# First products of eight f-tiles from scaled fp16 parts, and score visits that take two tiles, in a fused attention and feed-forward kernel on one core

## The chip, the cores and the metric

The kernel runs on one core of one Trainium2 chip. The metric is the device time in microseconds (us) of one execution, the median of several; lower is better. The kernel issues work on TensorE (PE in the rows; PEld is its weight load), VectorE (DVE), ScalarE (ACT), GpSimd (POOL), and DMAs from SyncE's queue (SP).

## What is computed

Linear attention memory and causal softmax attention are mixed by a gate, and the result goes through a feed-forward layer with softplus:

```python
# q, k, v: (4, 8, 576, 64); w_in: (512, 2048), w_out: (2048, 512); fp32 in and out
scores = where(causal, -1e9, 0.125 * q @ k.T)
a = exp(scores - max); a /= a.sum() + 1e-9
local = a @ v
q_p = elu(q) + 1
mem_out = (q_p @ M_prev) / (q_p @ z_prev + 1e-6)
x = sigmoid(beta) * mem_out + (1 - sigmoid(beta)) * local     # then (2304, 512)
out = softplus(x @ w_in) @ w_out
```

The weights arrive as 64-bit words and are turned into fp32 on the core ("decode").

## The kernel before

**Numbers as parts.** A fp32 operand of the feed-forward layer is kept as two fp32r parts, a high one and a low one (`hi`, `lo`), and a product is three matmuls: high by high, high by low, low by high (`in_pairs`, `out_pairs`, `mms`, L384). The attention weights and v are kept as two fp16 parts in most windows.

**Attention.** There are 16 units (4 batches by 4 pairs of heads), each cut into two windows: A has query chunks 0 and 1, B has chunks 2, 3 and the half chunk 4. `chunks` issues for each chunk a score visit on PE (fp32 matmuls of 64 by 64 quarters of the array, four at a time, L529; then a mask is added by two bf16 matmuls, L540 or L544), the row maxima (DVE, L549), the exponentials (ACT, L560), the high and low fp16 parts (POOL L617, DVE L621) and a transposing DMA. Chunk 4 has 64 queries per head; both heads stand in one 128-wide operand `qz` that POOL builds (L571), and its scores are two full-array matmuls of 288 columns (L533) and a mask (L535). A fp32 matmul stands as two records in the trace, so L533 has four per visit and L529 eight per chunk. Each visit uses one of the two score tiles of ring `s`. `v_prep` finds a power of two for v by a maximum, a tiny matmul pair against a constant (L749, L750) and a few scalar operations (L756, L758). `memory` does the linear memory (L800), `values` the product with v (L838) and the two parts of x (L867, L869).

**Feed-forward.** Its hidden units are 16 f-tiles of 128. f-tiles 0 to 6 are decoded during the attention and stay; for every finished block of x (8 blocks, 256 or 320 rows each, in turn) `fill` runs their first product (`hin`), softplus, and second product and puts the partial result into DRAM (`part`); this is also the work that PE does between attention steps. When the attention's buffers are free, f-tiles 7 to 15 are decoded into their place: one piece of `w_in` and one of `w_out` each, per piece four DVE steps (L349, L356, L360, L364) with one POOL step between them (L353), a cast on ACT (`hi`, L323) and a subtraction on POOL (`lo`, L317). `rest` then runs the last block with all 16 f-tiles and the seven others with f-tiles 7 to 15; there a first product of 12 matmuls (L384) alternates with a second product of 12 (L951).

**What sets the order.** A planner in the kernel (`Plan.run`) simulates the engines with the durations written at each `op`, ranks them by the tables at the top (`DEC`, `RK`, `SLOT`) and writes every engine's instructions in that order, so each engine's queue is fixed before the run. Where PE would idle early, it puts in dummy matmuls (L1034).

Of the kernel before, what the change touches and what calls it, by code (L numbers as in the profile page):

```python
# [10 lines left out]
F32 = mybir.dt.float32  # L11
# [83 lines left out]
class Plan:  # L95
# [5 lines left out]
    TURN = {"m": {"S": 60.0, "v": 160.0, "n": 70.0}, "f": {"v": 85.0}, "n": {"S": 30.0, "v": 80.0},  # L101
            "S": {"S": 85.0, "v": 80.0, "f": 90.0, "m": 90.0, "n": 90.0},
            "v": {"S": 80.0, "f": 90.0, "m": 90.0, "n": 90.0}}
# [44 lines left out]
    def run(self):  # L148
# [34 lines left out]
        def opens(o):  # L183
            t = 0.0
            for h in o.tiles:
                if h.ring is None or h.open:
                    continue
                if h.ring.free:
                    if h.before is not None and not h.before.open:
                        return None  # L190
                    if len(h.ring.opened) >= h.ring.bufs:
                        old = h.ring.opened[-h.ring.bufs]
# [80 lines left out]
def attn_softplus_moe(  # L273
# [25 lines left out]
    own = res.tile([128, 128], F32, name="own")  # L299
# [14 lines left out]
    LASTB = len(blocks) - 1  # L314

# [55 lines left out]
    def wpart(f, i, t):  # L371
        return W[f]()[:, i, t, :]

    def in_pairs(f, xh, kd, n):
        wh, wl = (W[f]()[:, 0, t, kd * 128:(kd + 1) * 128] for t in range(2))
        return [(wh, xh[:, 0, kd, :n]), (wh, xh[:, 1, kd, :n]), (wl, xh[:, 0, kd, :n])]

    def out_pairs(f, g, dm, n):
        wh, wl = (W[f]()[:, 1, t, dm * 128:(dm + 1) * 128] for t in range(2))
        return [(wh, g[:, 0, :n]), (wh, g[:, 1, :n]), (wl, g[:, 0, :n])]  # L380
# [5 lines left out]
    def consts():  # L386
# [11 lines left out]
        P.memset(own, 0.0)  # L398
        for h in range(2):
            P.memset(own[64 * h:64 * h + 64, 64 * h:64 * h + 64], 1.0)  # L400
# [9 lines left out]
        for r in range(2):  # L410
            V.tensor_copy(cinv4[64 * r:64 * r + 64, :], cv[64 * r:64 * r + 64, :, r])
# [12 lines left out]
    def ring(pool, tag, bufs, shape, dtype=F32):  # L424
# [6 lines left out]
        "sm": ring(ps_r, "sm", 1, [128, 512]),  # L431
# [11 lines left out]
        "PTA": ring(al, "PTA", 2, [128, 8, 256], F16), "PTB": ring(al, "PTB", 2, [128, 18, 320], F16),  # L443
# [8 lines left out]
    W = {}  # L452
    for f in range(NF):
# [3 lines left out]
        else:  # L457
            late, old = (wr, gone[ar]) if f < GA + 5 else (wl, gone[al])
            W[f] = Ring(late, f"w{f}", 1, [128, 2, 2, 512], F32R, old).new()
    QZ = [Handle(None, 0) for _ in range(2)]  # L460
    for i, h in enumerate(QZ):
        h.t = res.tile([128, 128], F32, name=f"qz{i}")
    X = [Handle(None, 0) for _ in blocks]
    PART = [Handle(None, 0) for _ in blocks]

    def decode(f, i, rank):
        s, tu = R["ws"].new(), R["wu"].new()
        hi, lo = (W[f], (i, 0)), (W[f], (i, 1))
# [4 lines left out]
        src = tu if WIDE else s  # L473
        for j, (e, d, port, fn) in enumerate(steps):
            if j < nv:
                op(e, d, rank, fn, r=[s], w=[tu], port=port)
            elif j == nv:
# [25 lines left out]
    def chunks(u, win, b, p, cs, ks):  # L503
# [14 lines left out]
        ss, nms, pts = (tiles(t) for t in ("s", "nm", "P"))  # L518
        l, r = R["l"].new(), R["rr"].new()

        def scores(js):
            for j in js:
                c, n, sv, qv, kv = cs[j], ns[j], ss[j](), q()[:, 130:], kk()
                cq = c * 128 - q0
                if c < 4:
                    for h in range(2):
                        rr = slice(64 * h, 64 * h + 64)
                        for e in range(0, 128, 64):
                            MM(sv[e:e + 64, h, so[j]:so[j] + n], lhsT=qv[rr, cq + e:cq + e + 64], rhs=kv[rr, :n],  # L529
                               start=j == js[0], stop=True, skip_group_check=True)  # L530
                else:
                    for i in range(2):
                        MM(sv[:, i, :288], lhsT=win.qz(), rhs=kv[:, 288 * i:288 * i + 288], start=True, stop=True)  # L533
            if m == 1:
                MM(sv[:, 1, 224:288], lhsT=identb, rhs=mask4, start=False, stop=True, skip_group_check=True)  # L535
                return
            for h in range(2):
                e = so[js[-1]] + ns[js[-1]]
                if len(js) == 2:
                    MM(sv[:, h, 0:512].rearrange("p (c n) -> p c n", c=2)[:, :, 0:128], lhsT=identb,  # L540
                       rhs=mask.unsqueeze(1).to_broadcast([128, 2, 128]), start=False, stop=True,
                       skip_group_check=True)
                else:
                    MM(sv[:, h, e - 128:e], lhsT=identb, rhs=mask, start=False, stop=True, skip_group_check=True)  # L544
# [22 lines left out]
        for j, c in enumerate(cs):  # L567
            k, s, nm, pt = ks[j], ss[j], nms[j], pts[j]
            if m == 1:
                win.qz = QZ[win.no // 2 % 2]  # L570
                op("POOL", 470, k + RK["qz"], lambda: P.tensor_tensor(  # L571
                    out=win.qz().rearrange("p (h q) -> p h q", h=2),
                    in0=q()[:, 130 + 256:130 + 320].unsqueeze(1).to_broadcast([128, 2, 64]),
                    in1=own.rearrange("p (h q) -> p h q", h=2), op=ALU.mult), r=[q], w=[win.qz])
            if not both or j == 0:
                js = range(len(cs)) if both else [j]
                op("PE", 1080 if both else (450, 660, 968, 1180, 1050)[c], k, lambda js=js: scores(js),
                   r=[q, kk] + ([win.qz] if m == 1 else []), mode="S" if m == 2 else "f",
                   w=[s] + ([(pt, "s")] if guard else []))
# [24 lines left out]
        for j, c in enumerate(cs):  # L604
            k, pt, phl = ks[j], pts[j], phls[j]
            if c < 4:
# [23 lines left out]
                op("SP", (1230, 1250, 1650, 2600)[c], k + RK["lo"], lambda j=j, c=c, nk=nk: SY.dma_start_transpose(  # L630
                    out=ptw()[:, 0:4 * nk, c * 128 - q0:c * 128 - q0 + 128],
                    in_=phls[j]()[:, ho[j]:ho[j] + nk * 512]),
                   r=[(phl, 4 * j + i) for i in range(4)], w=[(ptw, c)], dma=840 * nk)
# [29 lines left out]
            for h in range(2):  # L663
                op("SP", 1260, k + RK["lo"], lambda h=h: SY.dma_start_transpose(
                    out=ptw().rearrange("p (j h) q -> p j h q", h=2)[:, :, h, 256:320],
                    in_=phl()[64 * h:64 * h + 64, 0:1152]),
# [425 lines left out]
```

## Time and profile before

| | |
|---|---|
| median of 3 runs | 611.39 us (608.29 to 611.94) |
| the profiled execution | 610.6 us, of which the trace spans 608.8 |
| PE busy | 590.4 us (97%) |
| DVE, ACT, POOL busy | 353.0 (58%), 302.4 (50%), 173.0 (28%) |
| chain of work that ended last | 86% PE, of which first products (L384) 43%, second products of `rest` (L951) 21% |
| granted TensorE clock | 2.4 GHz (1.00) from start to end |

Rows of the windows view give, for a stretch, each engine's busy time and number of instructions. Rows of the timeline give start, duration (of the merged run) and count; matmuls are pipelined, so a run's pace is the distance between the starts of two runs divided by the count, not its duration.

### The profile page before, as it was taken

How to read it: one execution, taken by the hardware profiler on the slowest of the kernel's cores; microseconds unless marked ns; L12 is line 12 of the kernel's file. 1: busy time of each engine (PE TensorE's matmuls, PEld its weight loads, DVE VectorE, ACT ScalarE, POOL GpSimd, SP SyncE). 2: the span in 40 equal slices, each digit the busy share in tenths (PEclk: the TensorE clock that was granted, in tenths of full speed). 3: DMA queues.
4: the chain of work that ended last, by engine and by line, in shares of the span. 5: the costliest groups of instructions: out<-in, count | busy, mean ns of one | idle time of the engine just before them, and what ended most of it. 6: DMA issues, size and time to landing. Idle time of an engine off the chain costs nothing.

```text
span 608.8 us, 12824 instructions
## 1 busy us (share of the span) xinstructions
PE 590.4 (97%) x4866; PEld 528.5 (87%) x4866; DVE 353.0 (58%) x805; ACT 302.4 (50%) x854; POOL 173.0 (28%) x262
## 2 busy tenths in 40 slices
PE   6999999999989999989999999999999999999996
PEld 5676768787777787968799999999999999999996
DVE  6688888788877898868882776651212121212121
ACT  5758866666756785668743443432222222222221
POOL 3556533334433435326622343330000000000000
PEclk9999999999999999999999999999999999999999
DMA  8545559868999789967976643342314130522011
GB/s 314 190 125 178 181 157 220 195 195 183 205 180 210 192 187 200 177 164 163 169 123 182 214 137 106 105 145 98 105 36 133 48 132 6 167 71 70 1 44 35
DMA packets 129245, 87.41 MB, mean 144 GB/s; under 512 B 86176, under 2 KB 120992, under 8 KB 129184
## 3 DMA queue, kind: packets, MB, share of 16 engines
q1 hardware_dynamic: 129184, 86.60, 55.3%
q8 instruction: 38, 0.62, 0.4%
q14 instruction: 23, 0.19, 0.1%
HBM read 47.88 MB, written 18.22 MB: 109 GB/s over the span
## 4 chain that ended last, share of the span: by engine, by line
PE 86%; DMA 5%; DVE 4%; ACT 1%; SPq 1%; POOL 1%; issue 1%; DVEq 0%; ACTq 0%; POOLq 0%
PE h L384 43%; PE s L951 21%; PE s L529 6%; PE xp L838 4%; PE sm L800 3%; PE s L533 2%; DMA kA<-in_nat_dram 2%; PE xp L853 2%; PE xp L826 1%; PE s L544 1%; PE h L488 1%; DMA qA<-in_nat_dram 1%; PE s L715 1%; DVE nm L549 1%; DMA PTA<-PHL 1%
## 5 line engine op out<-in xcount | busy, mean ns | idle before, releaser
L384 PE MATMUL h<-xhl,w 128*128 128x256 f32 (+1 forms) x1536 | 228.1, 298 | 1.4 <-ACT pb L914 1.4
L384 PEld LDWEIGHTS h<-xhl,w 128*128 128x128 f32 x1536 | 210.4, 189 | 3.2 <-ACT pb L914 1.6
L317 DVE TENSOR_TENSOR g<-gl,g 128x256 fp32r<-128x256 f32 (+1 forms) x128 | 59.6, 470 | 162.8 <-ACT g L323 162.5
L888 ACT ACTIVATE gl<-h 128x256 f32<-128x256 f32 (+1 forms) x128 | 52.2, 410 | 179.2 <-PE h L384 176.8
L951 PE MATMUL s<-g,w 128*128 128x320 f32 (+1 forms) x948 | 139.3, 297 | 0.0
L951 PEld LDWEIGHTS s<-g,w 128*128 128x128 f32 x948 | 131.1, 188 | 0.0
L384 PE MATMUL h<-g,w 128*128 128x256 f32 (+1 forms) x588 | 87.1, 299 | 0.0
L384 PEld LDWEIGHTS h<-g,w 128*128 128x128 f32 x588 | 78.7, 189 | 0.7
L617 POOL TENSOR_SCALAR PHL<-P,rr 128x384 f16<-128x384 f32 (+3 forms) x100 | 57.4, 589 | 76.9 <-DVE rr L597 23.5
L560 ACT ACTIVATE P<-s,nm 128x256 f32<-128x256 f32 (+3 forms) x128 | 66.4, 526 | 5.2 <-DVE PHL L621 2.6
L549 DVE TENSOR_REDUCE nm<-s 128x2 f32<-128x768 f32 (+2 forms) x64 | 51.4, 818 | 13.9 <-PE s L540 7.3
L323 ACT CAST g<-gl 128x256 fp32r<-128x256 f32 (+1 forms) x128 | 55.1, 433 | 3.9
L621 DVE SCALAR_TENSOR_TENSOR PHL<-P,rr,PHL 128x384 f16<-128x384 f32 (+3 forms) x100 | 56.4, 599 | 0.8 <-POOL PHL L617 0.8
L317 POOL TENSOR_TENSOR w<-wu,w 128x512 fp32r<-128x512 f32 x23 | 30.5, 1329 | 29.2 <-ACT w L323 29.2
L353 POOL TENSOR_SCALAR wu<-wu 128x512 f32<-128x512 f32 x32 | 20.5, 643 | 43.7 <-DVE wu L349 38.3
L529 PE MATMUL s<-kB,qB 64*64 64x384 f32 (+1 forms) x256 | 31.4, 561 | 0.0
L838 PEld LDWEIGHTS <-vb 128*64 128x64 f16 x508 | 24.8, 110 | 7.1 <-issue 2.7
L360 DVE SCALAR_TENSOR_TENSOR wu<-ws,wu 128x512 int32<-128x512 int32 x32 | 26.6, 832 | 0.9
L792 POOL TENSOR_TENSOR ph<-ph,pe 128x320 f32<-128x320 f32 (+1 forms) x22 | 18.4, 838 | 30.8 <-ACT pe L784 18.9
L560 ACT ACTIVATION_READ_ACCUMULATOR P<-s,nm 128x1 f32 x128 | 25.5, 199 | 0.0
L323 ACT CAST w<-wu 128x512 fp32r<-128x512 f32 x29 | 17.9, 618 | 14.4 <-DVE wu L364 14.2
L678 POOL TENSOR_SCALAR P<-P,rr 128x256 f32<-128x256 f32 (+4 forms) x31 | 18.6, 613 | 20.5 <-DVE rr L597 10.7
(123 smaller groups left out, 643.2 us busy)
## 6 DMA issues: line engine op xcount, KB each, us to landing
ws<-in_w_in_dram SPq DMA_DIRECT2D x16, 512.0 KB, 3.6
ws<-in_w_out_dram SPq DMA_DIRECT2D x16, 512.0 KB, 3.5
va<-in_nat_dram SPq DMA_DIRECT2D x16, 320.0 KB, 3.9
xd<-xhl SPq DMA_DIRECT2D x16, 320.0 KB, 3.1
kB<-in_nat_dram SPq DMA_DIRECT2D x16, 288.0 KB, 3.8
xd<-xhl SPq DMA_DIRECT2D x16, 256.0 KB, 3.2
xhl<-xd SPq DMA_DIRECT2D x8, 512.0 KB, 4.6
xhl<-xd SPq DMA_DIRECT2D x6, 640.0 KB, 4.9
```

The costliest lines, as they stand in the source:

```text
L317: eng.tensor_tensor(out=out, in0=in0, in1=in1, op=ALU.subtract)
L323: A.copy(out, in_)
L360: V.scalar_tensor_tensor(out=ti(), in0=si(1), scalar=-0x40000000, in1=ti(), op0=ALU.bitwise_and, op1=ALU.bitwise_or)
L384: MM(out, lhsT=l, rhs=r, start=start and i == 0, stop=stop and i == len(pairs) - 1)
L529: MM(sv[e:e + 64, h, so[j]:so[j] + n], lhsT=qv[rr, cq + e:cq + e + 64], rhs=kv[rr, :n], start=j == js[0], stop=True, skip_group_check=True)
L549: V.tensor_reduce(out=nm()[:, 2 * j * both:2 * j * both + 2], in_=s()[:, :, so[j]:so[j] + n], op=ALU.max, axis=AX.X, negate=True)
L560: A.activation(out=pt()[:, po[j] + h * n:po[j] + h * n + n], in_=s()[:, h, so[j]:so[j] + n], func=AF.Softplus, scale=SCALE, bias=nm()[:, o ...
L617: P.tensor_scalar(out=o[:, :, 0, h, :], in0=src, scalar1=rs, scalar2=0.0, op0=ALU.mult, op1=ALU.add)
L621: V.scalar_tensor_tensor(out=o[:, :, 1, h, :], in0=src, scalar=rs, in1=o[:, :, 0, h, :], op0=ALU.mult, op1=ALU.subtract)
L838: MM(xp()[64 * h:64 * h + 64, lo:n], lhsT=vb()[:, vi, kc, 64 * h:64 * h + 64], rhs=ptw()[:, kc * 4 + t * 2 + h, lo:n], start=False, stop=( ...
L888: op("ACT", 170 + .833 * n, -1, lambda: A.activation(out=gl()[:, :n], in_=hp()[:, :n], func=AF.Softplus, scale=XSC), r=[hp], w=[gl])
L951: MM(bank(dm), lhsT=l, rhs=r, start=f == f0 and q == 0 and (not small or dm % 2 == 0), stop=f == NF - 1 and q == 2, skip_group_check=True)
```

## The change

- **First products of f-tiles 8 to 15** (`FINE`) use fp16 parts in place of fp32r parts. Each decoded `w_in` piece is scaled by a power of two found from its absolute maximum (`spread`: one DVE reduction, two tiny matmuls on PE, three one-column DVE operations); ACT writes the high fp16 part and DVE (not POOL) the low one. For each of the 8 blocks `halved` does the same to x: a reduction, the tiny matmuls, one ACT pass and two DVE passes over 4 times 256 or 320 columns, and one one-column DVE operation per f-tile that gives the softplus its inverse scale. Second products stay in fp32r, and so do f-tiles 0 to 7.
- **Chunk 4** of two neighbouring units is computed in one visit (`fours`), on 64 by 64 quarters, both units' quarters side by side; `qz` and its POOL operation are gone. The first unit's chunk 4 and values come after the second unit's chunk 3 scores.
- **Chunks 2 and 3** of 14 units are computed in one visit (`twos`). A visit of either kind takes both tiles of ring `s`.
- **Masks** are now written by the first matmuls of a visit, and the scores are added to them.
- The two transposing DMAs of a window A are one. The second memory product is split for 12 windows instead of 10 (`PHS`). Later `w_out` pieces have their own load and decode buffers (`ws2`, `wu2`). Some casts and evictions change engine; the planner's costs of switching PE between kinds of work (`TURN`) and the tables `DEC`, `RK`, `SLOT` have other numbers, so that the whole order is drawn anew.

The core of the diff:

```diff
+    def spread(src, out, rank, r, w, dur, axis):
+        sp = R["sm"].new(loose=True)
...
+        op("DVE", dur, rank, lambda: V.tensor_reduce(out=total(), in_=src(), op=ALU.max, axis=axis,
+                                                     apply_absolute_value=True), r=r, w=[(w, 3)])
+        op("PE", 80, rank, mn, r=[(w, 3)], w=[sp], mode="n")
+        op("DVE", 450, rank, scale, r=[sp], w=[(w, 1)])
...
     def decode(f, i, rank):
-        s, tu = R["ws"].new(), R["wu"].new()
+        s, tu = (R[g + "2" * (f > GA and i)].new() for g in ("ws", "wu"))
...
+                if j == nv:
+                    spread(raw, sf, rank, [src], WS[f], 690, AX.X)
+                    op("ACT", 640, rank, lambda: A.activation(out=wpart(f, 0, 0), in_=raw(), func=AF.Copy,
+                                                              scale=sf()[:, 1:2]), r=[src, (WS[f], 1)], w=[hi])
+                else:
+                    op("DVE", 740, rank, lambda: V.scalar_tensor_tensor(
+                        out=wpart(f, 0, 1), in0=raw(), scalar=sf()[:, 1:2], in1=wpart(f, 0, 0), op0=ALU.mult,
+                        op1=ALU.subtract), r=[src, hi, (WS[f], 1)], w=[lo], port=True)
...
+    def fours(wins, ks):
+        ss = [R["s"].new() for _ in wins]
...
+            for s in ss:
+                MM(s()[:, 1, 224:288], lhsT=identb, rhs=mask4, start=True, stop=False, skip_group_check=True)
+            for i in (1, 0):
+                for h in range(2):
+                    rr = slice(64 * h, 64 * h + 64)
+                    for s, w in zip(ss, wins):
+                        o = 64 * (h ^ w.odd)
+                        MM(s()[o:o + 64, i, :288], lhsT=w.q()[rr, 130 + 256:130 + 320],
+                           rhs=w.k()[rr, 288 * i:288 * i + 288], start=i == 0, stop=True, skip_group_check=True)
...
+    def halved(xh, n, rank):
...
+        spread(lambda: part(0), xs, rank, xr[:4], xs, 150 + 4.16 * n, AX.XY)
+        op("ACT", 260 + 3.36 * n, rank, lambda: A.activation(out=out(0), in_=part(0), func=AF.Copy,
+                                                             scale=xs()[:, 1:2]), r=xr[:4] + [(xs, 1)], w=[(x, 0)])
+        op("DVE", 215 + 4.16 * n, rank, lambda: V.scalar_tensor_tensor(
+            out=out(1), in0=part(0), scalar=xs()[:, 1:2], in1=out(0), op0=ALU.mult, op1=ALU.subtract),
+           r=xr[:4] + [(xs, 1), (x, 0)], w=[(x, 1)], port=True)
+        op("DVE", 215 + 4.16 * n, rank, lambda: V.scalar_tensor_tensor(
+            out=out(1), in0=part(1), scalar=xs()[:, 1:2], in1=out(1), op0=ALU.mult, op1=ALU.add),
+           r=xr[4:] + [(xs, 1)], w=[(x, 1)], port=True)
...
-        for f in range(f0, NF):
+        fs = [f for f in range(f0, NF) if f not in FINE] + FINE
+        for f in fs:
...
-            g = hin(f, xh, n, k + i)
+            g = hin(f, xh, n, k + i, fine if f in FINE else None)
...
+        if w == "B" and win.odd:
+            ks = [key(0), key(1)]
+            both = fours([prev[1], win], ks)
+            chunks(*prev, [4], ks[:1], both[0])
+            chunks(u, win, b, p, [4], ks[1:], both[1])
+            slot += 2
+            values(*prev, slot + RK["val"], xhs[2 * b + 1])
+        pre = twos(win, [key(0), key(1)]) if w == "B" and u.no in OPT["two"] else None
```

Two places of the order. First TensorE's queue in the last batch of the attention. Before: a visit for chunk 3 (tile `kB`, 512 columns), other work, and a visit for chunk 4 of one unit (with `qz`).

```order
L529 MATMUL s<-kB,qB 64x512 x4
L544 LDWEIGHTS identb
L544 MATMUL s<-mask,identb 128x128
L544 LDWEIGHTS identb
L544 MATMUL s<-mask,identb 128x128
L800 MATMUL sm<-qB,ph 128x130 x3
L826 MATMUL xp<-ident,mA 128x128 x2
L533 MATMUL s<-kB,qz_101 128x288 x2
L535 LDWEIGHTS identb
L535 MATMUL s<-mask_67,identb 128x64
L384 MATMUL h<-xhl,w_94 128x320 x6
```

Now, at the corresponding place: the visit for chunk 4 of two units, feed-forward work, and a visit for chunks 2 and 3 of the next unit.

```order
L561 LDWEIGHTS identb
L561 MATMUL s<-mask_67,identb 128x64
L561 LDWEIGHTS identb
L561 MATMUL s<-mask_67,identb 128x64
L567 MATMUL s<-kB,qB 64x288 x8
...
L582 LDWEIGHTS identb
L582 MATMUL s<-mask,identb 128x128
...
L589 MATMUL s<-kB,qB 64x384 x4
L589 MATMUL s<-kB,qB 64x512 x4
L387 MATMUL h<-xhl,w_98 128x320 x6
```

One visit with two masks ahead of it stands where two with a mask behind each stood (of the four L582 masks one pair of rows is shown).

Second, VectorE's queue where the later weights are decoded, while PE runs the last `fill`. Before (`wu` and `ws` are a piece being decoded, `g` a result of the feed-forward layer, `xhl` the last unit's x):

```order
L869 SCALAR_TENSOR_TENSOR xhl<-xp,sc,xhl 128x320
L356 TENSOR_SCALAR wu<-wu 128x512
L360 SCALAR_TENSOR_TENSOR wu<-ws,wu 128x512
L317 TENSOR_TENSOR g<-gl,g 128x256
L364 SCALAR_TENSOR_TENSOR wu<-ws,wu 128x512
L317 TENSOR_TENSOR g<-gl,g 128x256
L356 TENSOR_SCALAR wu<-wu 128x512
```

Now, for f-tile 8 (`wsc` its scale, `v_5235` its fp16 parts, `iv` the inverse scale; `wu_5197` is the next piece):

```order
L495 TENSOR_REDUCE wsc<-wu 128x1
L317 TENSOR_TENSOR g<-gl,g 128x256
L349 TENSOR_SCALAR wu_5197<-ws_5051 128x512
L317 TENSOR_TENSOR g<-gl,g 128x256
L489 TENSOR_SCALAR wsc<-sm 128x1
L491 TENSOR_SCALAR wsc<-wsc 128x1
L493 TENSOR_SCALAR wsc<-wsc 128x1
L989 TENSOR_SCALAR iv<-wsc,xs 128x1
L356 TENSOR_SCALAR wu_5197<-wu_5197 128x512
L360 SCALAR_TENSOR_TENSOR wu_5197<-ws_5051,wu_5197 128x512
L317 TENSOR_TENSOR g<-gl,g 128x256
L524 SCALAR_TENSOR_TENSOR v_5235<-wu,wsc,v_5235 128x512
```

VectorE has a reduction, four one-column operations and a subtraction more per f-tile, and it waits between L495 and L489 for the tiny matmuls on PE (`sm`), which stand at a fixed place in PE's queue, in the middle of a second product:

```order
L1073 MATMUL s<-g,w_5259 128x320 x6
L484 LDWEIGHTS mean
L484 MATMUL sm<-least,mean 128x1
L485 LDWEIGHTS mean
L485 MATMUL sm<-wsc,mean 128x1
L1073 MATMUL s<-g,w_5259 128x320 x6
```

Before, a first product of 12 matmuls followed a second product of 12 here, and PE's queue held nothing of the decode.

## Rows read from the trace of the kernel before

**Rows 1.** Windows: us, then each engine's busy time (and instructions), granted clock.

```profile
15.20:61.00 45.80, 43.50 (x328) 30.87 (x330) 36.82 (x85) 33.34 (x102) 25.75 (x44) 1.00 0.50 164
61.00:122.00 61.00, 59.31 (x530) 46.59 (x527) 51.22 (x125) 41.56 (x124) 24.66 (x38) 1.00 0.73 189
331.00:366.00 35.00, 35.00 (x279) 34.89 (x276) 25.92 (x44) 15.10 (x35) 14.44 (x15) 1.00 0.49 160
366.00:402.00 36.00, 36.00 (x248) 36.00 (x247) 23.17 (x41) 13.38 (x28) 15.55 (x16) 1.00 0.31 103
```

**Rows 2.** Source L1034, the dummies: durations min/median/max in ns, first and last start.

```profile
L1034 PE MATMUL sm<-ident x44: 268/275/373, 15.9 to 72.6; 128*128 128x122 f32 x44
```

**Rows 3.** PE's waits from 15.2 to 61 us: total, times, longest.

```profile
PE s L533 <- ACT P L560: 0.2, 1, 0.2
```

**Rows 4.** Timeline of PE in the tail: start, duration, line, tiles, count.

```profile
472.07 1.58 PE L384 MATMUL h<-xhl,w 128*128 128x256 f32 x12
473.49 1.58 PE L951 MATMUL s<-g,w 128*128 128x256 f32 x12
...
543.75 1.92 PE L384 MATMUL h<-xhl,w 128*128 128x320 f32 x12
545.51 1.60 PE L951 MATMUL s<-g,w 128*128 128x256 f32 x12
```

**Rows 5.** Windows of L838 alone, 18 fp16 matmuls of 320 columns.

```profile
106.39:107.61 1.22, 1.22 (x18) 1.22 (x20) 1.00 0.59 111
```

**Rows 6.** Timeline of PE: visits for chunks 2 and 3, and one for chunk 4.

```profile
207.38 0.88 PE L529 MATMUL s<-kB,qB 64*64 64x384 f32 x8
...
208.29 1.12 PE L384 MATMUL h<-xhl,w 128*128 128x320 f32 x6
209.34 1.09 PE L529 MATMUL s<-kB,qB 64*64 64x512 f32 x8
210.36 0.28 PE L544 MATMUL s<-mask,identb 128*128 128x128 bf16 x2
210.46 0.39 PE L384 MATMUL h<-xhl,w 128*128 128x320 f32 x1
...
215.01 0.75 PE L384 MATMUL h<-xhl,w 128*128 128x320 f32 x4
215.60 1.13 PE L533 MATMUL s<-kB,qz 128*128 128x288 f32 x4
216.57 0.19 PE L535 MATMUL s<-mask,identb 128*128 128x64 bf16 x1
216.60 0.69 PE L384 MATMUL h<-xhl,w 128*128 128x320 f32 x3
```

**Rows 7.** Timeline of PE: the tiny matmul pair, and the end of a product with v.

```profile
117.27 0.18 PE L749 MATMUL sm<-least,mean 128*128 128x1 bf16 x1
117.31 0.16 PE L750 MATMUL sm<-sc,mean 128*128 128x1 bf16 x1
117.33 0.54 PE L384 MATMUL h<-xhl,w 128*128 128x320 f32 x2
...
172.91 1.72 PE L838 MATMUL xp<-PTB,vb 128*64 128x320 f16 x28
174.56 0.62 PE L384 MATMUL h<-g,w 128*128 128x256 f32 x3
175.02 0.88 PE L384 MATMUL h<-xhl,w 128*128 128x256 f32 x6
```

**Rows 8.** Source views of DVE's lines: durations min/median/max in ns, first and last start.

```profile
L349 DVE TENSOR_SCALAR wu<-ws x32: 396/420/1392, 5.2 to 399.7; 128x512 int32<-128x512 int32 x32
L356 DVE TENSOR_SCALAR wu<-wu x32: 406/421/1515, 6.5 to 400.9; 128x512 int32<-128x512 int32 x32
L360 DVE SCALAR_TENSOR_TENSOR wu<-ws,wu x32: 680/693/1671, 7.0 to 402.5; 128x512 int32<-128x512 int32 x32
L740 DVE TENSOR_REDUCE sc<-va x12: 802/812/822, 66.7 to 248.7; 128x1 bf16<-128x640 f32 x12
L651 DVE SCALAR_TENSOR_TENSOR PHL<-P,rr,PHL x13: 723/744/765, 95.1 to 316.4; 128x512 f16<-128x512 f32 x13
```

**Rows 9.** Timeline in the decode: a subtraction on POOL beside DVE.

```profile
341.39 1.34 POOL L317 TENSOR_TENSOR w<-wu,w 128x512 fp32r<-128x512 f32 x1 [1.06 <-ACT w L323]
341.62 1.67 DVE L360 SCALAR_TENSOR_TENSOR wu<-ws,wu 128x512 int32<-128x512 int32 x1
```

More of the change, by code (lines that the diff above doesn't have):

```diff
@@ L188, in opens @@
                 if h.ring.free:
-                    if h.before is not None and not h.before.open:
+                    if h.before is not None and not h.before.open and h.before not in o.tiles:
                         return None
-                    if len(h.ring.opened) >= h.ring.bufs:
-                        old = h.ring.opened[-h.ring.bufs]
+                    i = len(h.ring.opened) + sum(g.ring is h.ring and not g.open for g in o.tiles[:o.tiles.index(h)])
+                    if i >= h.ring.bufs:
+                        old = h.ring.opened[i - h.ring.bufs]
                         if old.left:
@@ L451, in attn_softplus_moe @@
     R["pp"] = Ring(wl, "pp", 2, [128, 4, CAP], F32, gone[al])
-    W = {}
+    R["x16"] = Ring(wl, "x16", 2, [128, 2, 4, CAP], F16, gone[al])
+    R["wu2"] = Ring(wl, "wu2", 2, [128, 512], F32, gone[al])
+    R["ws2"] = Ring(wl, "ws2", 2, [128, 1024], F32, gone[al])
+    R["xs"] = ring(moe, "xs", 2, [128, 4])
+    R["iv"] = ring(moe, "iv", 2, [128, NF])
+    WS = {f: Handle(None, 0) for f in FINE}
+    wsc = res.tile([128, NF, 4], F32, name="wsc")
+    W, W16 = {}, {}
     for f in range(NF):
@@ L473, in decode @@
         src = tu if WIDE else s
+        late = f in FINE and not i
         for j, (e, d, port, fn) in enumerate(steps):
@@ L516, in tiles @@
             return [t if both or not j else R[tag].new() for j in range(len(cs))]
-        ss, nms, pts = (tiles(t) for t in ("s", "nm", "P"))
+        if done:
+            (ss, pts), nms = done, tiles("nm")
+        else:
+            ss, nms, pts = (tiles(t) for t in ("s", "nm", "P"))
         l, r = R["l"].new(), R["rr"].new()
         def scores(js):
[L522 to L536, printed above, removed]
@@ L568, in chunks @@
             k, s, nm, pt = ks[j], ss[j], nms[j], pts[j]
[L569 to L575, printed above, removed]
+            if not done and (not both or j == 0):
                 js = range(len(cs)) if both else [j]
-                op("PE", 1080 if both else (450, 660, 968, 1180, 1050)[c], k, lambda js=js: scores(js),
-                   r=[q, kk] + ([win.qz] if m == 1 else []), mode="S" if m == 2 else "f",
+                op("PE", 1075 if both else (450, 660, 928, 1142)[c], k, lambda js=js: scores(js), r=[q, kk], mode="S",
                    w=[s] + ([(pt, "s")] if guard else []))
@@ L930, in rest @@
                    r=[(X[bi], p) for p in range(4)], w=[(xh, 4 * t + p) for p in range(4)], dma=5.8 * n)
+        fine = halved(xh, n, k + count[0] - LAG if f0 else 500.0) if FINE else None
         pp = R["pp"].new()
```

190 lines of the change are left out of this document (134 added, 56 removed).

## The prediction

> **What bounds the kernel now.** I read the page first: PE is busy 97% of the span and makes up 86% of the chain that ended last, so the question is where PE is really the limit. The windows view answers by stretch [rows 1]. From 61 us on PE is busy over 97% of every stretch and from 331 us on without a gap, at the granted clock of 1.00 (2.4 GHz): what PE saves there, the kernel can save. Before that it is not so: from 15.2 to 61 us PE is idle for 2.3 of 45.8 us, and it also runs dummies, 44 records of 0.27 us, the last at 72.6 us [rows 1, 2]. In that part the decode of f-tiles 0 to 6 and the first softmaxes set the pace, so I count no gain there. The second thing to see is DVE: 84% busy from 61 to 122 us, and only 25.92 + 23.17 = 49.1 of 71 us (69%) in the decode of the later f-tiles from 331 to 402 us [rows 1]. That is the room that the change uses up.
>
> **fp16 first products.** In the tail a run of 12 fp32r matmuls is followed by the next after 1.42 us for 256 columns and 1.76 us for 320: 0.118 and 0.147 us each [rows 4]. The only fp16 matmuls with many columns are those with v: 18 of 320 columns start in 1.22 us [rows 5], two at a time in the two halves of the array, so 9 pairs at 0.1356 us. That is 2 ns over 320 columns at 2.4 GHz; for 256 the same gives 0.109 us. There are 8 f-tiles x 8 blocks x 12 = 768 of these matmuls, half of each width: 384 x (0.147 - 0.1356) + 384 x (0.118 - 0.109) = 7.9 us. Bounds: at exactly one column per cycle (0.1333, 0.1067) it would be 9.6; nothing, if the pace belongs to the full 128 by 128 array and not to the number format. A loss I exclude: the loads of fp32r weights are busy for the whole of the tail (36.00 of 36.00 us [rows 1]) and still stay behind the matmuls. I take 7.9.
>
> **Chunk 4 by pairs.** Before, a visit takes 1.00 us from its first matmul to the next work [rows 6], and the matmul behind a mask comes late: behind chunk 2 six matmuls of 0.147 end at 209.17, and the next visit starts at 209.34, 0.17 us that I split evenly between leaving the mask and entering the quarters. So 1.08 us, 2.16 for two units. One pass of 288 columns takes 0.97 / 4 = 0.243 us on the full array; on the quarters, chunk 3 takes 1.12 and chunk 2 0.91 us, 0.21 more for two passes of 128 columns, which is the same price per column. A new visit has two small masks (0.06), the entry (0.09, and 0.03 for the first pass), four passes (0.97), and the way back from quarters to the full array. For that the nearest row is the end of a product with v: 1.65 us for columns worth 1.52, and then three matmuls of 0.118 in 0.46 us [rows 7], together 0.2 us. Sum 1.35; saved 0.8 per pair. Bounds: with a cheap way back 0.9; if the two units' quarters do not run together, eight passes, and the pair loses 0.16.
>
> **Chunks 2 and 3 in one visit.** Before 0.91 + 1.12 + 2 x 0.17 = 2.37 us. After: four masks at 0.06, entry 0.12, passes 2 x (0.32 + 0.43) = 1.5, way back 0.2: 2.06. Some of the visits were already neighbours, so 0.28 saved, with bounds 0.1 and 0.4. In a window A the mask only changes its place: the entry is saved and the dearer way back paid, 0.08 us lost (0 to 0.1).
>
> Eight pairs, 14 double visits and 16 windows A; the first batch (2, 4 and 4) lies in the stretch that PE does not bound. What counts is 6 x 0.8 = 4.8, 10 x 0.28 = 2.8, and 12 x 0.08 = 1.0 lost.
>
> **What is added on PE.** A tiny matmul pair takes 0.06 us [rows 7] and the matmul behind it is 0.08 late as behind a mask: 16 x 0.14 = 2.2 us. Two more windows with a split memory product are four more fp32 matmuls of 130 columns in two passes at 0.82 ns per column: 0.9 us.
>
> **What is added on DVE.** A piece's four steps are 0.42, 0.42, 0.69 and 0.69 us (the fourth as the third) [rows 8], 4.4 us per f-tile. New per f-tile are a reduction over 512 columns (from 0.81 for 640: 0.68), four or more one-column operations (estimated at 0.15), and the low part (0.74) [rows 8]: 2 us, 16 for eight. `halved` for the last block is a reduction and two passes over 1280 columns, some 4.6 us by the same rows. I summed DVE's queue in the new order from the last unit's x to the last fp16 part of f-tile 15: 16 pieces 35.5, 22 subtractions for g 10.4, eight reductions 5.4, eight low parts 6.0, 45 one-column operations 6.7, `halved` 6.1: 70 us. PE's queue from the same point to the first product of f-tile 15 holds 168 matmuls of 0.118 (19.8 us), 288 of 0.147 (42.3) and 84 in fp16 (11.4): 73.5 us. So DVE must be busy 95% of the time. PE waits earlier than that, since the tiny matmuls stand in its queue at fixed places: those for f-tile 8 after 11 us and for f-tile 9 after 20, where DVE's own work alone is 10 to 11 and 19 us. Each delay of DVE there is a stall of PE, and all matmuls queue behind it. Such delays exist: beside a subtraction on POOL a DVE step of 0.69 took 1.67 us [rows 9]; half of these subtractions go away. For f-tiles 11 to 15 DVE is 2 to 5 us ahead. I take 2.5 us of stall, with bounds 0 and 12 (a microsecond for each remaining POOL subtraction, and the chain from reduction to low part never covered). In the later blocks `halved` is hidden: about 6 us of DVE work in a block of some 25 us of PE. The removed `qz` operations on POOL, the merged transposes and the casts on other engines lie beside PE work, and I count nothing for them.
>
> **Sum.** -7.9 - 4.8 - 2.8 + 1.0 + 2.2 + 0.9 + 2.5 = -8.9 us. From the span of 608.8 that gives 599.9; with the 1.8 us around it 601.7; the median of the runs is 0.8 above the profiled execution, so **602.5 us**.
>
> **Rivals.**
> *fp16 paces like fp32r.* The products with v run in halves of the array, not on all of it, so the row is not the same case. Then the 7.9 us are gone: 610.4, no change. The Trainium skill has a rule for this side (TensorE: Matmul & The Clock Gate, "Weight-path perf modes"): the array handles one element per cell and cycle whatever its width. By that rule alone the format would bring nothing; but fp32r at 0.147 is 13 ns above that rate in the trace, so the rule does not describe the fp32r rows, and I give it 1 in 10.
> *DVE becomes the bound of the decode.* PE then stalls at one tiny pair after the other, 5 to 12 us instead of 2.5: 605 to 612. For it speaks the 95%; against it that DVE gets ahead from f-tile 11 on. 15 in 100.
> *Slower: both score tiles at once.* `fours` and `twos` take both tiles of ring `s`, so a visit cannot start before the softmax of the previous pair has left both, while until now one was filled as the other was read. Of 22 such visits each may cost PE a wait; at 0.4 us each the gain is gone, from 0.7 us on the kernel is over 1% slower (618 and more). The wait is there for the taking: maxima and exponentials of a pair last several microseconds. Against it: today PE waits for the exponentials 0.2 us in 46 [rows 3], and feed-forward matmuls stand between nearly all visits. 8 in 100.
> *All of it arrives.* Columns at the full rate, no stall in the decode, and the first batch gains too (2 x 0.8 + 4 x 0.28): 602.5 - 1.7 - 2.5 - 2.7 = 595.6. 15 in 100.
>
> **From these to the numbers.** The forecast has 52 in 100, its own range 598 to 607. About 1% is what a measurement of this kernel can tell from no change, so faster means under 605.3 and slower over 617.5. Faster: the last rival and all of the forecast but its upper end, 0.61. Same: that end (0.06), the first two rivals: 0.31. Slower: 0.08. The range 594 to 612 takes in the full-gain case and the two that end near no change, and leaves the slow one and some tails out.
>
> **What would show it.** In the tail, 12 fp16 matmuls of 320 columns should take 1.63 us and of 256 columns 1.31, start to start; 1.76 and 1.42 would make the first rival right. A visit for chunk 4 should take 1.35 us for two units; 2.3 means that the quarters took turns. PE's waits after the attention should name DVE's scales at the tiny pairs with 2 to 3 us in all; over 5 means the DVE rival. Waits of score visits for P or `nm` above 0.2 us each would show the slow one. A block of the tail without any of this should be shorter by about 1 us (96 x 0.011), less 0.14.

## The result: 604.24 us, and the profile after

The changed kernel takes **604.24 us** (median of 8 runs, 602.55 to 607.2) against 611.07 us for the kernel before in the same comparison (8 runs, 608.29 to 614.84): a ratio of 0.9882, with a 95% interval of 0.9858 to 0.9905. The forecast was 602.5. Its profiled execution took 603.7 us, of which the trace spans 601.9. The eight executions differ with the clock: three with a mean granted clock of 0.999 took 602.55 to 603.58 us, the five with 0.993 to 0.995, the profiled one among them, 603.68 to 607.2.

One sentence ahead of this was half wrong about the program: the scores of the first unit's chunk 4 come before the second unit's chunks 2 and 3, not behind its chunk 3; only the first unit's values come behind them. No term of the sum rested on it.

Windows of the changed kernel, columns as in [rows 1]; the attention ends (start of the last matmul with v) at 331.6 us before and at 323.0 now, and I call that point T0:

```profile
61.00:100.00 39.00, 36.16 (x298) 26.90 (x295) 32.41 (x75) 25.16 (x68) 16.11 (x23) 0.96 0.46 147
100.00:122.00 22.00, 21.03 (x222) 16.78 (x222) 17.95 (x43) 15.23 (x57) 10.65 (x20) 1.00 1.04 244
122.00:323.00 201.00, 199.20 (x1915) 167.47 (x1916) 167.84 (x403) 133.07 (x407) 83.26 (x120) 1.00 0.89 190
...
366.00:402.00 36.00, 34.68 (x244) 29.66 (x242) 33.03 (x77) 15.44 (x28) 10.40 (x11) 1.00 0.38 125
```

Three things stand out against [rows 1]. DVE went from 23.17 to 33.03 of 36 us between 366 and 402 us, and PE now has gaps there. From 61 to 100 us PE is idle for 2.8 us and its clock is below 2.4 GHz for part of the time (0.96). And the dummies grew from the 44 of [rows 2] to

```profile
L1170 PE MATMUL sm<-ident x78: 265/275/372, 12.3 to 101.5; 128*128 128x122 f32 x78
```

The tail, timeline of PE, to be read beside [rows 4] by the starts of the runs:

```profile
450.69 1.80 PE L387 MATMUL h<-x,v 128*128 128x320 f16 x12
452.22 2.03 PE L1073 MATMUL s<-g,w 128*128 128x320 f32 x12
454.09 1.80 PE L387 MATMUL h<-x,v 128*128 128x320 f16 x12
...
466.49 1.49 PE L387 MATMUL h<-x,v 128*128 128x256 f16 x12
467.73 1.66 PE L1073 MATMUL s<-g,w 128*128 128x256 f32 x12
469.24 1.48 PE L387 MATMUL h<-x,v 128*128 128x256 f16 x12
```

Twelve fp16 matmuls of 320 columns reach the next run after 1.53 us, and the fp32r run behind them needs 1.87 instead of 1.76. Neither number is a price by itself. The twelfth fp16 matmul of that run is this row:

```profile
452.19 0.30 PE L387 MATMUL h<-x,v 128*128 128x320 f16 x1
```

So the step from one fp16 matmul to the next is (452.19 - 450.69) / 11 = 0.136 us, and the first fp32r matmul is recorded only 0.03 us behind the start of the last fp16 one; what the first run seems to save there, the second seems to lose. What counts is first and second product together: 3.40 us against 3.52, and 2.75 against 2.84 for 256 columns. A visit for chunk 4 of two units, and one for chunks 2 and 3, to be read beside [rows 6]:

```profile
150.00 2.44 PE L387 MATMUL h<-g,w 128*128 128x320 f32 x15
152.28 0.23 PE L561 MATMUL s<-mask,identb 128*128 128x64 bf16 x2
152.45 1.20 PE L567 MATMUL s<-kB,qB 64*64 64x288 f32 x16
153.58 0.94 PE L883 MATMUL sm<-qB,ph 128*128 128x130 f32 x6
...
156.25 0.90 PE L387 MATMUL h<-g,w 128*128 128x320 f32 x5
156.99 0.40 PE L582 MATMUL s<-mask,identb 128*128 128x128 bf16 x4
157.31 1.74 PE L589 MATMUL s<-kB,qB 64*64 64x384 f32 x16
158.98 1.72 PE L929 MATMUL xp<-PTB,vb 128*64 128x320 f16 x28
```

Fifteen matmuls of 0.147 from 150.00 end at 152.20, so the pair takes 1.38 us (1.41 as a mean over the visits, with what follows); the other visit 2.00 us here and 2.10 where a full-array product follows. And the decode of the last two f-tiles, where PE now waits:

```profile
396.65 1.15 PE L1073 MATMUL s<-g,w 128*128 128x320 f32 x6
398.04 1.52 PE L1073 MATMUL s<-g,w 128*128 128x320 f32 x6 [0.24 <-ACT g L323]
399.39 0.18 PE L484 MATMUL sm<-least,mean 128*128 128x1 bf16 x1
...
399.46 1.12 PE L1073 MATMUL s<-g,w 128*128 128x320 f32 x6
401.23 0.45 PE L387 MATMUL h<-x,v 128*128 128x320 f16 x2 [0.65 <-ACT v L521]
402.05 1.53 PE L387 MATMUL h<-x,v 128*128 128x320 f16 x10 [0.37 <-DVE v L524]
```

The bracket gives only the idle part. By starts (the distance to the next row, less what the matmuls need), six matmuls of 0.147 (0.88 us) took 1.39, 1.35 and 1.77 us, and two of 0.128 took 0.82: 0.51 + 0.47 + 0.89 + 0.56 = 2.4 us late. With 0.6 us at 329 us (PE waits for the softplus, `gl`) and 0.15 elsewhere the stalls behind T0 come to 3.1 us.

### The profile page after: what moved, and what is told of

Read it like the earlier page. It is cut to its first block, busy times and chain, and to the rows that moved or that the text cites. A ratio compares the mean times of both kernels' runs of the same rounds, so it can differ in the third digit from the quotient of the medians.

```text
span 601.9 us, 13130 instructions
## 1 busy us (share of the span) xinstructions
PE 583.1 (97%) x5004; PEld 499.7 (83%) x5004; DVE 408.8 (68%) x959; ACT 314.7 (52%) x856; POOL 163.2 (27%) x239
## 4 chain that ended last, share of the span: by engine, by line
PE 83%; DMA 3%; DVE 3%; ACT 1%; POOL 1%; issue 0%; SPq 0%; DVEq 0%; POOLq 0%; ACTq 0%
PE h L387 43%; PE s L1073 21%; PE xp L929 5%; PE sm L883 3%; PE s L589 3%; PE s L634 2%; DMA PTB<-PHL 2%; PE xp L909 1%; PE s L567 1%; PE s L802 1%; DMA kA<-in_nat_dram 1%; PE xp L943 1%; PE h L538 1%; DVE nm L640 1%; DMA qB<-in_nat_dram 0%; PE s L582 0%
## 5 line engine op out<-in xcount | busy, mean ns | idle before, releaser
L1073 PE MATMUL s<-g,w 128*128 128x320 f32 (+1 forms) x948 | 146.3, 303 | 0.3 <-ACT g L323 0.2
L387 PE MATMUL h<-xhl,w 128*128 128x256 f32 (+1 forms) x768 | 114.1, 300 | 0.6 <-ACT gl L1007 0.6
L387 PEld LDWEIGHTS h<-xhl,w 128*128 128x128 f32 x768 | 104.6, 189 | 4.3 <-issue 1.9
L387 PE MATMUL h<-x,v 128*128 128x320 f16 (+1 forms) x768 | 105.1, 287 | 1.0 <-ACT v L521 0.7
L1007 ACT ACTIVATE gl<-h,iv 128x320 f32<-128x320 f32 (+1 forms) x64 | 32.0, 500 | 114.6 <-PE h L387 114.3
L387 PEld LDWEIGHTS <-v 128*128 128x128 f16 x768 | 69.9, 98 | 21.3 <-ACT v L521 0.9
L651 ACT ACTIVATE P<-s,nm 128x128 f32<-128x128 f32 (+3 forms) x128 | 66.4, 525 | 2.3
L1007 ACT ACTIVATE gl<-h 128x256 f32<-128x256 f32 (+1 forms) x64 | 25.9, 409 | 40.6 <-PE h L387 39.7
L317 POOL TENSOR_TENSOR w<-wu,w 128x512 fp32r<-128x512 f32 x15 | 21.8, 1455 | 54.3 <-ACT w L323 54.2
L646 ACT ACTIVATE nm<-nm 128x2 f32<-128x2 f32 (+2 forms) x64 | 12.8, 201 | 26.6 <-DVE nm L640 17.1
```

The costliest lines, as they stand in the source:

```text
L317: eng.tensor_tensor(out=out, in0=in0, in1=in1, op=ALU.subtract)
L387: MM(out, lhsT=l, rhs=r, start=start and i == 0, stop=stop and i == len(pairs) - 1)
L651: A.activation(out=pt()[:, po[j] + h * n:po[j] + h * n + n], in_=s()[:, h, so[j]:so[j] + n], func=AF.Softplus, scale=SCALE, bias=nm()[:, o ...
L1007: op("ACT", 170 + .833 * n, -1, lambda: A.activation(out=gl()[:, :n], in_=hp()[:, :n], func=AF.Softplus, scale=iv()[:, f:f + 1] if fine el ...
L1073: MM(bank(dm), lhsT=l, rhs=r, start=f == fs[0] and q == 0 and (not small or dm % 2 == 0), stop=f == fs[-1] and q == 2, skip_group_check=True)
```

## The experiments

Each states the time as a median and as a ratio to the kernel before on the same chip; the changed kernel stands at 604.24 and 0.9882.

### fp32r again (e1_fp32r)

```diff
- 'fine': {8, 9, 10, 11, 12, 13, 14, 15}
+ 'fine': set()
```

> All f-tiles in fp32r again, the rest as in the changed kernel; the last weight pieces have no buffers of their own. The trace of the changed kernel gives fp16 6.9 us on PE (3.40 against 3.52 us for a first and a second product of 320 columns, 2.745 against 2.84 for 256), less 16 tiny pairs at 0.15 (2.4 us) and 3.1 us of stalls after the attention: net 1.4 us. If that is right, 605 to 607 us against 604.2. Rival, fp16 carries the whole gain: 610 to 611. Rival, the decode stalls have nothing to do with the scales: they stay at about 3 us, and the time is 608 to 610.

Measured: 606.35 us, ratio 0.9903 (0.987 to 0.9935). T0 is the same to 0.1 us and no wait of PE is left behind it. fp16 with its search of scales nets 2.1 us by the medians and 1.3 by the ratios. The two intervals overlap, so these times alone do not show a gain; the spans behind T0 in the next experiment give 281.4 - 278.9 = 2.5 us. The forecast's -7.9 + 2.2 + 2.5 had -3.2.

### Scales as constants (e4_fixed_scale)

```diff
-        op("DVE", dur, rank, lambda: V.tensor_reduce(out=total(), ...
-        op("PE", 80, rank, mn, r=[(w, 3)], w=[sp], mode="n")
-        op("DVE", 450, rank, scale, r=[sp], w=[(w, 1)])
...
+            P.memset(out()[:, 1:2], 2.0 ** (7 - e))
+            P.memset(out()[:, 2:3], 2.0 ** (e - 7))
```

> The powers of two are constants written by POOL: this leaves out the search for the scales (the maxima, the tiny matmuls, the one-column operations), for weights and x. If DVE's longer way per f-tile makes the stalls, they vanish with the reductions: 2.4 us of tiny pairs and 3.1 of stalls, 598 to 599 us. If the stalls come from somewhere else (loads, ACT), only the tiny pairs go: 601 to 602.

Measured: 598.82 us, ratio 0.9777 (0.9747 to 0.9808). This run and the one before price the two halves of the edit, since T0 is the same in all three (323.0 to 323.2). Windows from T0 to the end: of fp32r again, of constants, of the changed kernel:

```profile
323.10:604.50 281.40, 276.70 (x2084) 276.37 (x2078) 89.81 (x167) 83.73 (x194) 32.53 (x33) 1.00 0.29 91
```

```profile
323.20:597.20 274.00, 269.24 (x2084) 246.78 (x2078) 123.28 (x239) 99.54 (x202) 27.14 (x37) 1.00 0.30 94
```

```profile
323.00:601.90 278.90, 272.15 (x2116) 247.84 (x2112) 143.14 (x319) 99.82 (x202) 24.16 (x25) 0.99 0.29 92
```

The first two run the same 2084 matmuls, 768 of them in the other format: **fp16 alone is worth 281.4 - 274.0 = 7.4 us**. The search costs 278.9 - 274.0 = 4.9 us: the 3.1 us of stalls and 1.8 us for the 16 tiny pairs. A pair costs 0.15 us where fp32r matmuls follow it, nine times, and about 0.07 where an fp16 run follows, seven times, since that run does not start late:

```profile
447.23 0.18 PE L484 MATMUL sm<-least,mean 128*128 128x1 bf16 x1
...
447.30 1.79 PE L387 MATMUL h<-x,v 128*128 128x320 f16 x12
```

This form beats both kernels, but its constants are right only for inputs of this size.

### Twice the reduction on DVE (e7_double_max)

```diff
-        op("DVE", dur, rank, lambda: V.tensor_reduce(out=total(), ...
+        def most():
+            for _ in range(2 if axis == AX.X else 1):
+                V.tensor_reduce(out=total(), ...
```

> The order of the changed kernel; only the reduction over 512 columns that finds each weight piece's largest value runs twice, 8 x 0.68 = 5.4 us more on DVE and nothing more on PE. Theory (DVE is the limit of the late decode, 33.0 of 36 us busy from 366 to 402 us, and PE's 3.1 us of stalls come from it): the stalls after the attention grow by 2.5 to 5 us and the time by as much, 606.5 to 609 us. Rival (the stalls are delays of single steps, and DVE has room between them): the time stays at 604 within 1 us and the stalls within 1 us of 3.1.

Measured: 607.86 us, ratio 0.9948 (0.9928 to 0.9968): 3.6 us more. T0 stays (323.3), and from there to the end it takes 282.3 us instead of 278.9. PE's waits behind T0:

```profile
PE h L387 <- ACT v L524: 0.9, 1, 0.9
PE sm L485 <- DVE wsc L497: 0.9, 3, 0.3
PE s L1076 <- DVE g L317: 0.7, 1, 0.7
```

Of 5.4 us on DVE 3.4 come through to the end: DVE is what PE waits for in the late decode, with 2 us of room.

### The fp16 tiles chosen otherwise (e10_fine_8_13, e12_fine_10_15)

```diff
- 'fine': {8, 9, 10, 11, 12, 13, 14, 15}
+ 'fine': {8, 9, 10, 11, 12, 13}
```

> fp16 parts with scales for f-tiles 8 to 13 only; 14 and 15 are decoded as before. On PE 16 first products go back to fp32r, by the two traces 0.12 us (320 columns) and 0.095 us (256) each: 1.7 us more, and two tiny pairs less, 0.3 us. On DVE 2 x 2 us of the last tiles' work falls away. Theory (DVE's queue from the last block of attention to the last weight piece is some 78 us and ends later than PE can wait, so the stalls stand at the last tiles): the 2.4 us of stalls at f-tiles 14 and 15 vanish, 604.2 + 1.7 - 0.3 - 2.4 = 603.2 us, and the last decode step ends about 74 us after the last product with v instead of 78. Rival (the stalls belong to single late steps): they stay or move to f-tiles 12 and 13, 605 to 606 us.

Measured: 621.75 us, ratio 1.0173 (1.0141 to 1.0204), far from both. `rest` takes `[f not in FINE] + FINE`, so tiles 14 and 15 moved ahead of 8 in PE's queue, while DVE still decodes them last. The timeline of PE and a window show the price:

```profile
386.69 0.90 PE L387 MATMUL h<-xhl,w 128*128 128x320 f32 x2 [7.28 <-ACT w L323]
...
394.83 3.03 PE L1073 MATMUL s<-g,w 128*128 128x320 f32 x10 [0.91 <-POOL w L317]
397.66 2.93 PE L387 MATMUL h<-xhl,w 128*128 128x320 f32 x12
```

```profile
394.00:398.00 4.00, 3.17 (x12) 3.17 (x13) 3.93 (x4) 0.62 (x1) 2.27 (x2) 0.50 0.00 0
```

PE waits 7.3 us for one piece and runs at 1.2 GHz (0.50) behind it: the ten matmuls from 394.83 on reach the next run after 2.83 us, where at 2.4 GHz they need 1.47. The run says nothing on the question, and much on what an order of use that differs from the order of decode costs. So the same number of tiles, the right way round:

```diff
+ 'fine': {10, 11, 12, 13, 14, 15}
```

> fp16 parts with scales for f-tiles 10 to 15, so that the two tiles without them (8 and 9) are decoded first and used first; a block takes the tiles with fp16 parts last, so leaving out 14 and 15 instead had put these two ahead of 8 in PE's queue and behind 13 in DVE's. 16 first products go back to fp32r: 8 x (0.12 + 0.095) = 1.7 us more, two tiny pairs less, 0.3 us. DVE has 4 us less to do between the last unit and the last piece. Theory (the amount of DVE's work against PE's work ahead of f-tiles 14 and 15 makes the stalls): the last decode step ends about 74 us after the last product with v instead of 78, the 2.4 us of stalls at 14 and 15 go, 604.2 + 1.4 - 2.4 = 603.2 us. Rival (single late steps make them, whatever the sum): the stalls stay near 3 us, 605.6 us.

Measured: 603.29 us, ratio 0.9863 (0.9837 to 0.9888). PE's waits behind T0 are down to two, the one for the softplus (`gl`) and one more:

```profile
PE h L387 <- ACT gl L1007: 0.6, 1, 0.6
PE sm L485 <- DVE wsc L495: 0.3, 1, 0.3
```

The stalls at 14 and 15 are gone, and the time is the 603.2 expected; it cannot be told from the changed kernel's. One part missed: the last low part ends 77.7 us behind T0 (79.0 in the changed kernel), not 74. PE no longer waits for the last pieces; what paces them stays open.

### The low part on POOL (e11_pool_low)

```diff
+                    if f >= 12:
+                        op("POOL", 2600, rank, low, r=[src, hi, (WS[f], 1)], w=[lo], port=True)
+                        continue
```

> For f-tiles 12 to 15 POOL makes the low part (two operations over 512 columns: scaling in place and a subtraction) in place of DVE, which loses 4 x 0.74 = 3.0 us of work. Theory (the number of DVE's microseconds is the limit, and POOL is free): the last decode step on DVE ends about 75 us after the last product with v, the stalls fall from 3.1 to under 1 us, 601.5 to 602.5 us. Rival (POOL's operations of two inputs stretch DVE's own, as the 1.67 us in place of 0.69 in the trace of before, and POOL's two operations are slow): the stalls at f-tiles 12 to 15 stay or grow, 604 to 609 us.

Measured: 612.8 us, ratio 1.0036 (1.0014 to 1.0058): the rival, and more. DVE has fewer busy microseconds, 29.90 instead of 33.03 of 36 from 366 to 402 us, and the decode is later all the same: the last low part ends 85.9 us behind T0 instead of 79.0. Each of these low parts is now two operations in a row on POOL (0.78 and 1.49 us for one of them, 0.75 on DVE), and a DVE step beside them is stretched. Timelines of POOL and, behind it, of DVE:

```profile
386.43 1.49 POOL L527 TENSOR_TENSOR v<-wu,v 128x512 f16<-128x512 f32 x1
```

```profile
386.82 1.65 DVE L360 SCALAR_TENSOR_TENSOR wu<-ws,wu 128x512 int32<-128x512 int32 x1
```

The 1.65 us in place of 0.69 is [rows 9] again, now beside the new subtraction. PE's two longest waits behind T0:

```profile
PE sm L485 <- DVE xs L495: 2.8, 1, 2.8
PE h L387 <- POOL v L527: 1.9, 1, 1.9
```

The longest is not at one of the four tiles, as the rival had it, but at the search of a following block's x, which stands among the late pieces in DVE's queue. The granted clock is 0.62 from 400 to 404 us behind the second wait, and T0 comes 1.3 us later; both are part of the 8.6 us.

### Chunk 4 twice (e5_double_c4)

```diff
-            for i in (1, 0):
+            for t, i in ((0, 1), (0, 0), (1, 1), (1, 0)):
```

> The order of all instructions is that of the changed kernel; only the score matmuls of each chunk 4 pair run twice, so chunk 4's scores are doubled before the softmax (a change of what is computed) and each of the 8 pair visits takes four passes of 288 columns more: 4 x 0.243 = 0.97 us, by the changed kernel's rows 1.41 + 0.97 = 2.38 us for a visit. It prices a microsecond of PE in the attention. Theory (PE bounds the attention except in the first batch): 6 x 0.97 = 5.8 us more than the changed kernel, 610 us. Rival 1 (the first batch is on the path as well): 8 x 0.97 = 7.8, 612. Rival 2 (the visits are partly hidden behind softmaxes or transfers): under 4 us more, under 608.

Measured: 610.36 us, ratio 0.9988 (0.9972 to 1.0004): 6.1 us more by the medians, 6.5 by the ratios. Each visit is longer by just what was added, 2.27 us from its first mask where it took 1.30:

```profile
155.79 0.23 PE L561 MATMUL s<-mask,identb 128*128 128x64 bf16 x2
...
158.06 0.94 PE L883 MATMUL sm<-qB,ph 128*128 128x130 f32 x6
```

So PE's time in the attention is the kernel's time from the second batch on (5.8 us), one for one to within a microsecond or so. In the trace the first two visits count in part: the first second product of the feed-forward starts at 96.3 us instead of 94.9, 1.4 of the 1.9 us put in ahead of it. With 5.8 that makes 7.2; T0 comes 6.9 us later there.

### Chunks 2 and 3 apart (e2_no_twos, e8_twos_later)

```diff
- 'two': {0, 1, 2, 3, 4, 5, 6, 7, 8, 9, 10, 11, 14, 15}
+ 'two': set()
```

> Chunks 2 and 3 in visits of their own again, pairs for chunk 4 stay. A double visit took 2.10 us in the changed kernel, the two single ones 2.37 before. If only the ten units behind the first batch count, 2.7 us slower: about 607. If all fourteen count, 608. Rival, a visit that takes both score tiles makes the softmax wait: the single visits give something back, and the time is 604 or less.

Measured: 610.12 us, ratio 0.9969 (0.9949 to 0.9989), 5.9 us more, where the visits alone (14 x 0.27) make 3.8: T0 comes 4.8 us later, and from T0 on it takes 1.3 us more (280.2), with more waits in the decode (1.1 us each for the scaled high part, the low part and g). That second part was not expected. Only the first batch apart:

```diff
+ 'two': {4, 5, 6, 7, 8, 9, 10, 11, 14, 15}
```

> Chunks 2 and 3 share a visit in the later batches only; in the first batch (4 units) they are apart, as before. The planner then writes a new order. Theory (the shared visits of the first batch hold back the first softmaxes and the decode behind them, which is why the first second-product of the feed-forward came at 94.9 us instead of 92.2, after 1.9 us of idle PE and a spell at 1.2 GHz): the first second-product at about 92 us, less idle time of PE between 60 and 100 us, and the time 601 to 603 us. Rival (that stretch depends on the order as a whole, or on the windows A and the pairs): the same 604 us, or more, with the first second-product at 94 us or later.

Measured: 608.25 us, ratio 0.9954 (0.9934 to 0.9974). The start came as expected, the time did not: the first second product starts at 92.3 us as before the change (92.2), and the granted clock from 61 to 100 us is back at 1.00. But T0 is at 327.7, and PE's waits from 340 to 420 us are

```profile
PE h L387 <- ACT v L521: 2.2, 2, 2.0
PE s L1073 <- ACT g L323: 1.6, 2, 1.4
PE h L387 <- DVE v L524: 1.4, 2, 0.9
PE s L1073 <- DVE g L317: 0.8, 2, 0.6
```

The windows view to T0 and from T0 shows where the time went:

```profile
122.00:327.70 205.70, 204.97 (x1965) 173.67 (x1963) 168.25 (x402) 135.99 (x411) 81.11 (x120) 1.00 0.89 184
327.70:605.20 277.50, 266.17 (x2062) 240.83 (x2056) 141.55 (x316) 97.22 (x195) 25.01 (x25) 1.00 0.29 92
```

Between 122 us and T0 the new order puts 5.8 us more of PE's work (204.97 against 199.20) and leaves 6.0 us less behind T0 (266.17 against 272.15). DVE's decode with its search takes 77 to 79 us from T0 in this order, in the one without shared visits and in the changed kernel's, so less of PE's work covers it, and the idle time behind T0 grows by 4.6 us (277.50 - 266.17 against 278.90 - 272.15), where the start had gained 2.6, some 1.6 of them the clock's (see the first batch, below).

### Both (e9_fixed_later)

The edits of constants and of the first batch apart, together.

> The scales are constants (the search for the largest value is left out: reductions, tiny matmuls, one-column operations; the constants suit inputs of this size), and the first batch's chunks 2 and 3 are apart. If the two gains add up: 598.8 less the 1 to 3 us of the other edit, 596 to 598 us. If the redrawn order loses what the edit gains: 598.8 to 601 us.

Measured: 597.53 us, ratio 0.9781 (0.9756 to 0.9807), not to be told from constants alone. With the search gone PE has no wait behind T0 (329.3 here, and 267.0 us from there), so the 6 us of waits came from the search. Against constants alone the earlier start brings 1.3 us by the medians and nothing by the ratios: that it is worth anything by itself is not shown.

### Chunk 4 by single units (e3_single_c4)

`fours` and its calls put back to one visit per unit, with `qz` on POOL and the old scale table; everything else as changed.

> Chunk 4 of each unit alone again, with qz from POOL and full-array matmuls, right after the unit's own chunks 2 and 3. A pair visit took 1.41 us, two single ones 2.16. Six pairs that count: 4.5 us slower, about 608.7; all eight: 610. Rival, the later values of a pair's first unit cost as much as the visits save: 604 to 606.

Measured: 629.83 us, ratio 1.0283 (1.025 to 1.0316). The tables of the order were made for pairs, and the redrawn order starts the first second product at 101.1 us, runs 110 dummies and leaves PE idle for 3.6 to 4.8 us in each of the stretches from 16 to 60, from 60 to 100 and from 200 to 250 us. It prices the misfit, not the visit; the price of the visit rests on the rows above.

## Why the prediction was right, and where it was not

**fp16 first products: -7.9 forecast, -7.4 measured** by two kernels that differ in little else (-6.9 by the rows of the tail). The pace was as read from the products with v: 0.136 us a step for 320 columns, and a first and a second product together take 3.40 and 2.75 us, where the forecast's 1.63 + 1.76 and 1.31 + 1.42 make 3.39 and 2.73. The sign that the prediction named, 1.63 and 1.31 us start to start, reads 1.53 and 1.24 instead, only because the first fp32r record begins early. The rule of the Trainium skill (TensorE: Matmul & The Clock Gate, "Weight-path perf modes") that the array takes one element per cell and cycle whatever the width would have made this zero. The trace does not agree with it for fp32r at these widths (0.147 us against 0.136 for the same 320 columns), and the rival that rested on it is out. Why fp32r is slower no run here shows.

**Chunk 4 by pairs:** 1.38 to 1.41 us against 1.35, so the quarters of two units do run side by side; 0.75 to 0.78 saved per pair against 0.8. **Chunks 2 and 3:** 2.0 to 2.1 against 2.06. **Windows A:** 0.10 lost against 0.08. **Tiny pairs:** 1.8 us against 2.2, since seven of the sixteen stand ahead of an fp16 run, which does not start late. The rest is as forecast, and the doubled chunk 4 shows that such microseconds count nearly in full once the first batch is past.

**The stall of the decode: 2.5 forecast, 3.1 measured, and in another place.** DVE's work was right: 70 us summed, 69.4 us busy in the 79.0 between T0 and the last low part. The step that failed is the one on when it falls due: I expected PE to wait at the tiny pairs of f-tiles 8 and 9 and saw DVE 2 to 5 us ahead from 11 on; PE waits at 14 and 15 instead, with g, the search and the last block's x in DVE's queue between the pieces. Doubling the reduction (+3.4 us) puts the cause on DVE, and without the search the stalls are gone.

**The first batch** was to bring nothing. In the profiled execution it lost 2.7 us up to the first second product of the feed-forward, and the last early piece is decoded at 93.7 us instead of 84.6. PE waits 1.9 us for DVE at a dummy and then runs part of the time at 1.2 GHz. Rows of before, of the changed kernel, and of f-tiles 10 to 15 (e12_fine_10_15), which issues the same matmuls there (the last row of the second and third is one of the windows view):

```profile
92.20 1.68 PE L384 MATMUL h<-g,w 128*128 128x256 f32 x12
```

```profile
82.31 1.38 PE L1170 MATMUL sm<-ident 128*128 128x122 f32 x10 [1.92 <-DVE mA L896]
94.86 1.68 PE L387 MATMUL h<-g,w 128*128 128x256 f32 x12
84.00:88.00 4.00, 4.00 (x22) 3.94 (x22) 1.74 (x8) 1.65 (x3) 0.69 (x1) 0.62 0.67 250
```

```profile
82.09 1.38 PE L1170 MATMUL sm<-ident 128*128 128x122 f32 x10 [1.92 <-DVE mA L896]
93.08 1.68 PE L387 MATMUL h<-g,w 128*128 128x256 f32 x12
84.00:88.00 4.00, 3.92 (x29) 2.80 (x29) 2.83 (x10) 2.48 (x6) 0.69 (x1) 1.00 0.64 234
```

The wait is the same, but the clock fell only in the changed kernel's execution: from the dummy to the second product it takes 12.55 us there and 10.99 in the other. So some 1.6 of the 2.7 us are the clock's, and belong to single executions rather than to the order. None of this was foreseen. That the decode and the first softmaxes set the pace of the first part was not shown either: [rows 3] has one of four lines for 15.2 to 61 us, and the largest are dummies that wait for DVE's `mA` and `mB`, 3.3 us.

Time came back where I had counted nothing either: between 100 us and T0 PE waits 2.8 us, mostly for transfers, where it waited 6.5 before:

```profile
100.00:331.60 231.60, 225.15 (x2066) 188.48 (x2065) 182.32 (x445) 150.35 (x459) 93.11 (x143) 1.00 0.86 184
```

These two, +2.7 and -3.7, nearly cancel, and that is luck. The terms of the forecast as measured are -7.4 - 4.6 - 2.7 + 1.2 + 1.8 + 0.9 (not measured apart) + 3.1 = -7.7 us, with these two -8.7; the ratio is worth -7.2, and the two traces differ by 6.9. The 1.5 us and more that are left I cannot account for.

The slow rival (score visits waiting for both tiles) did not happen: no wait of a score visit for P or `nm` over 0.2 us is in the trace.

## What to carry to other kernels

A format that is faster on PE is worth what is left after the work that prepares it: here 7.4 us of matmul time shrank to some 2 us, because finding the scales costs PE 1.8 us of its own and keeps DVE busy in the one stretch where PE then waits for it, 3.1 us. Time saved ahead of a stretch that another engine paces is only kept if work is left to cover that stretch: in the run with the first batch apart, filling the gaps early took 6 us of cover away, and the waits grew by more than the start had gained. And an order of use must follow the order of preparation: two tiles moved ahead against it cost 17.5 us.

## What was not expected of the hardware

Where the format changes, the starts in the rows mislead: an fp16 run seems 0.10 us faster and the fp32r run behind it 0.11 us slower than they are, and only the two together (3.40 us, 0.01 more than the sum of their steps) are a price. A wait that stops PE for some microseconds can cost more than itself: where two tiles stood in the wrong order, the granted clock was 0.50 (1.2 GHz) from 382 to 398 us, and PE's matmuls behind the wait of 7.3 us ran at that pace. In the first batch a wait of 1.9 us was followed by 0.62 from 84 to 88 us in the changed kernel, and the same wait by 1.00 with f-tiles 10 to 15.
